# Attention and a gated feed-forward layer in f32: the first layer over 1024 tokens in 49 products instead of twice 26, two chunks of the second layer side by side, and the third batch's attention moved beside chunk 0

## Chip, cores and metric

One core of a Trainium2 chip. The time is the device time of one launch in microseconds (us). Engines: PE is TensorE (matmuls), PEld its weight loads, DVE is VectorE, ACT is ScalarE, POOL is GpSimd, SP is SyncE (it issues DMAs here).

## What is computed

```python
def _attn_ref(q, k, v, g_norm):                      # q, k, v: (8, 8, 576, 64)
    kv = np.einsum('bhsd,bhse->bhde', k, v)
    out = np.einsum('bhsd,bhde->bhse', q, kv)
    rms = np.sqrt(np.mean(out * out, axis=-1, keepdims=True) + 1e-06)
    return (out / rms * g_norm).astype(np.float32)
...
def _moe_ref(x, w_gate, w_val, w_out):               # x: (4608, 512), d_ff = 1536
    gate = 1.0 / (1.0 + np.exp(-(x @ w_gate)))
    val = x @ w_val
    return (gate * val @ w_out).astype(np.float32)
```

The attention output, heads side by side, is x: 8 batches of 576 tokens. The weights come in as f64, read as pairs of 32-bit words.

## The kernel before

**Tiles.** x is held transposed, features on partitions, in a ring of three chunks of `G` = 512 tokens (`xT_ring`). There are `NG` = 9 chunks, while batches have 576 tokens, so batch b's attention has to be done shortly before chunk b. d_ff is cut into `N3` = 3 groups `j`, each of four blocks of 128.

**Chunk 0** is computed plainly. `plain` (L618) makes gate and value with 512-column matmuls, ACT takes the sigmoid, DVE multiplies; `second` (L853) is the second layer. Beside it run the conversion of the weights to f32 (`convert`, L195 to L235: 18 units of 1024 columns, five DVE steps and two ACT steps each, staged by SP through three buffers), the attention of batch 1, the set-up of batch 2, and on POOL the sums of the first layer's weights (`w1_sums`, L770, 28 of 256 columns for each `j`). The order is written out by hand: `places` names steps after the n-th matmul (CV is one conversion step, LL loads k and v, W0 and W1 are weight sums, `t` turns q, `u` multiplies, `s` sums squares, `r` takes the root, `n` normalizes, `x` turns the result and sends it into the ring by SP's DMAs).

**Chunks 1 to 8** use a bilinear scheme. `PRODUCTS1` lists 26 products, which stand for a 4 x 4 by 4 x 2 block product (32 plain ones). Each names a PSUM bank region, a weight form, an x form and the steps after it. `first_layer_fast` (matmuls L977, two of 256 columns a product) runs the list for each `j`; `combine` gives a plain copy out of PSUM to ACT (L943) and every sum or difference to DVE (L947); POOL multiplies gate and value (L939; the last ones of `j` = 2 on DVE). Five PSUM banks go round (`free`). `second_layer_fast` (L1079) runs 26 products over sums of h (`h_sums`, L752, on POOL, some for `j` = 2 on DVE) and forms of the output weights. Forms of x are DVE subtractions (`x_sums`, L875 and L877), 18 per chunk. In chunk 1 the first layer reads its weight forms where they were made and SP stores them (`keep_w1`); from chunk 2 on POOL's DMA queue loads them back in four granules per `j` (L799), and 15 of the second layer's forms (L1035).

**Attention of batch c + 1** is spread over chunk c's products by `feed`: `kv_mm` and `u_mm` (L400, L450) on TensorE between products, turns (L416, L477), sums of squares (L462) and norms (L470) on DVE, square and root on ACT. `u_mm` borrows one of the five banks and a tile of three more.

Every engine works through its instructions in program order, so a step that is emitted between two products stands in that place in its engine's queue.

Of the kernel before, what the change touches and what calls it, by code (L numbers as in the profile page):

```python
# [20 lines left out]
def kernel(  # L21
# [55 lines left out]
    raw_ctx = tc.tile_pool(name="raw", bufs=1, side="right")  # L77
    raw = raw_ctx.__enter__()

    first_ctx = tc.tile_pool(name="first", bufs=4)  # L80
    first = first_ctx.__enter__()

# [4 lines left out]
    def load_kv(n):  # L87
        if n >= NE:
            return
        b, h0 = n // NHP, 2 * (n % NHP)  # L90
        for name, src in (("k", k), ("v", v)):
            t = first.tile([NP, 2, NJ * HD], FP32, tag=name, name=name)
            nc.sync.dma_start(out=t, in_=src[b, h0:h0 + 2].rearrange("h (p j) d -> p h (j d)", j=NJ))
            pairs[n][name] = t

    def load_q(n):
        h0 = 2 * n
        t = first.tile([NP, NJ, 2, HD], FP32, tag="q", name="q")
# [6 lines left out]
    def load_q_run(b, m):  # L105
        if b >= B:
            return
        if b == 1:
            t = h_main[2 - m].rearrange("p s c -> p (s c)")[:, 4 * NT * P - QW:4 * NT * P]
# [13 lines left out]
    def load_late(b):  # L123
# [5 lines left out]
        for n in range(NHP):  # L129
            for name, src in (("k", k), ("v", v)):  # L130
                mains[n, name] = t = kv_place(len(mains))
                (nc.gpsimd if b == 2 else nc.sync).dma_start(out=t.rearrange("p (h c) -> p h c", h=2),
                                  in_=src[b, 2 * n:2 * n + 2, 0:S4].rearrange("h (p j) d -> p h (j d)", j=NK4))
        rest = kv_place(len(mains))
        for i, src in enumerate((k, v)):
            for r in range(2):
                (nc.sync if b == 1 else nc.gpsimd if b == 2 else nc.scalar).dma_start(out=rest[PH * r:PH * r + PH, GH * i:GH * i + GH].rearrange("p (h d) -> p h d", d=HD),
# [11 lines left out]
    def load_unit(u, halves=(0, 1)):  # L149
# [3 lines left out]
        if 0 in halves:  # L153
            staged[u] = raw.tile([P, 2, DM], I64, tag="st", name="st", bufs=NST)
# [15 lines left out]

    EXP_OFF = 896
    one = const.tile([P, 1], FP32, name="one")
    nc.vector.memset(one, 1.0)
    exp_off = const.tile([P, 1], FP32, name="exp_off")
    nc.vector.memset(exp_off, -EXP_OFF * 2.0 ** 23)

    def convert(u):
# [24 lines left out]
        def s1():  # L202


            if u < 15:
                t = raw.tile([P, UW], U32, tag="cz", name="cz", bufs=2)
            else:
                t = at_ps()[:, 0:2].rearrange("p r c -> p (r c)").bitcast(U32)
            d["p"] = p = by_block(t)
# [50 lines left out]
    w1 = const.tile([P, N3, 4 * NMT, 2, P], FP32, name="w1")  # L260
    w2 = const.tile([P, NFT, DM], FP32, name="w2")
# [6 lines left out]
    kv_ahead = const.tile([P, NRUN, 2, HD], FP32, name="kv_ahead")  # L268
# [12 lines left out]
    NX = 3  # L281
    xT_ring = const.tile([P, NMT, NX * G], FP32, name="xT")
    xT = {c: xT_ring[:, :, G * (c % NX):G * (c % NX + 1)] for c in range(NG)}

    def chunk(c):
        return xT[c]
# [87 lines left out]
    def feed(b):  # L374
# [3 lines left out]
        def kv_mm(at, lent):  # L378
# [5 lines left out]
            def tails(first):  # L384
                for e in range(2):
                    for m in range(NRUN):
                        for g in range(2):
                            rs, c = slice(PH * m, PH * m + PH), HD * (2 * g + e)
                            nc.tensor.matmul(ps[m][HD * g:HD * g + HD, e], rest[rs, c:c + HD],
                                             rest[rs, GH + c:GH + c + HD], start=first and e == 0, stop=not first,  # L390
                                             skip_group_check=True)

            if b != 2:
                tails(True)
            for m in range(NRUN):
                for e in range(2):
                    for j in range(NK4):
                        for g in range(2):
                            c = slice(NK4 * HD * e + HD * j, NK4 * HD * e + HD * j + HD)
                            nc.tensor.matmul(ps[m][HD * g:HD * g + HD, e], mains[2 * m + g, "k"][:, c],  # L400
                                             mains[2 * m + g, "v"][:, c], start=(b == 2 and e == 0 and j == 0),
                                             stop=(b != 2 and j == NK4 - 1), skip_group_check=True)
            if b == 2:
                tails(False)

        def kv_set_aside():
            for m in range(NRUN):
                nc.scalar.copy(out=kv_ahead[:, m], in_=d["kv"][m])
            d["kv"] = [kv_ahead[:, m] for m in range(NRUN)]
# [13 lines left out]
        def heads_run(m):  # L423
# [13 lines left out]
            def u_mm(first=()):  # L437
                at = at_ps()
                d["u"] = u = at.rearrange("p r c -> p (r c)")[:, 0:2 * S]
                i_ = 4 if b == 1 else free.popleft()  # L440
# [13 lines left out]
            def u_square():  # L454
                i_, lent, to = d["lent"]
                nc.scalar.copy(out=to, in_=lent)
                if b > 1:
# [15 lines left out]
            def x_turn(i):  # L473
# [7 lines left out]
                for j in range(2):  # L481
                    for e in range(2):
                        p0, p1 = HD * e + QB * j, HD * e + QB * i
                        s0 = 0
                        while s0 < S // 2:
                            o = (S * b + S // 2 * j + s0) % (NX * G)
                            n_ = min(NX * G - o, S // 2 - s0)
                            nc.sync.dma_start(out=xT_ring[p1:p1 + QB, 2 * m:2 * m + 2, o:o + n_],
# [8 lines left out]
            if b == 1:  # L497
# [710 lines left out]
```

## Time and profile before

| | |
|---|---|
| runs | 999.07 and 1000.05 us, median 999.56 |
| profiled execution | 999.39 us, span 997.6, granted TensorE clock 1.000 |
| busy | PE 989.5, PEld 814.3, DVE 718.4, POOL 616.7, ACT 343.3 us |
| chunk 0 and start | to 156.67 us |
| a chunk with attention, first layer | 72.6 us |
| a chunk without, first layer | 67.34 us |
| second layer of a chunk | 33.68 us |
| DMA | 194.96 MB, mean 195 GB/s |

A stage's times are read from the chain of work that ended last and from busy times by stage. An f32 matmul leaves two records. Busy time of PE counts matmuls whose ends are modelled, so the gaps in the chain say more than the share. In a group's row the durations stand as busy time and mean in ns, then the engine's idle time ahead of the group and what ended it.

### The profile page before, as it was taken

The page shows a single profiled execution, that of the slowest core. Times are in us where ns is not written, and L with a number is a line of the kernel's source. Part 1 is how long each engine was busy: PE and PEld are TensorE (multiplying, and loading weights), DVE is VectorE, ACT ScalarE, POOL GpSimd, SP SyncE. Part 2 cuts the span into 40 slices and gives each one's busy share as a digit, 9 for nine tenths or more (in the row PEclk, how much of TensorE's full clock was granted, in tenths as well). Part 3 has the DMA queues.
Part 4 walks back from the last instruction along what each step waited for, and adds up shares of the span by engine and source line. Part 5 has one row for each costly group of instructions (what it writes and reads, how often), then busy time and mean ns, then how long its engine had stood idle before and what let it go on. Part 6 is the DMA issues. An engine that isn't in the chain of part 4 may idle for free.

```text
span 997.6 us, 16584 instructions
## 1 busy us (share of the span) xinstructions
PE 989.5 (99%) x5958; PEld 814.3 (82%) x5958; DVE 718.4 (72%) x1185; ACT 343.3 (34%) x621; POOL 616.7 (62%) x991
## 2 busy tenths in 40 slices
PE   8999999999999999999999999999999999999998
PEld 7455447888888888888888888888888888888887
DVE  4989999898768766784777576866687566756672
ACT  4576323661144213530344124511442133213320
POOL 1339997798259635865286708771686359734963
PEclk9999999999999999999999999999999999999999
DMA  9986415763989568746975677656954455545514
GB/s 273 304 235 207 150 42 148 232 217 100 295 269 291 154 195 273 198 157 200 277 225 162 198 212 260 181 168 198 279 178 146 147 188 197 159 148 168 215 49 123
DMA packets 149522, 194.96 MB, mean 195 GB/s; under 512 B 79840, under 2 KB 121696, under 8 KB 149440
## 3 DMA queue, kind: packets, MB, share of 16 engines
q0 software_dynamic: 22512, 116.41, 35.3%
q1 hardware_dynamic: 120848, 75.66, 26.9%
q10 hardware_dynamic: 6080, 1.84, 0.8%
q8 instruction: 47, 0.77, 0.3%
q14 instruction: 35, 0.29, 0.1%
HBM read 160.04 MB, written 25.56 MB: 186 GB/s over the span
## 4 chain that ended last, share of the span: by engine, by line
PE 91%; DVE 4%; ACT 2%; DMA 1%; issue 1%; SPq 0%; DVEq 0%; ACTq 0%
PE mm L977 54%; PE mm L1079 27%; PE mm L618 3%; PE mm L853 3%; PE at L450 2%; DVE w L222 1%; DVE cz L226 1%; DVE w L195 1%; PE at L400 1%; ACT sqs L494 1%; DMA v<-in_v_dram 1%; PE mm L400 1%; DVE cz L210 0%; ACT w L200 0%; DMA xT<-xTs 0%
## 5 line engine op out<-in xcount | busy, mean ns | idle before, releaser
L977 PE MATMUL mm<-xs,w 128*128 128x256 f32 x1428 | 331.2, 379 | 0.0
L977 PEld LDWEIGHTS mm<-xs,w 128*128 128x128 f32 x1428 | 270.9, 190 | 37.0
L977 PE MATMUL mm<-xT,w 128*128 128x256 f32 x948 | 230.5, 380 | 0.0
L977 PEld LDWEIGHTS mm<-xT,w 128*128 128x128 f32 x948 | 179.6, 190 | 25.0 <-issue 0.5
L799 POOL DMA_DIRECT2D w<-kept x84 | 46.9, 559 | 203.0 <-PE mm L977 199.5
L947 DVE TENSOR_TENSOR sg<-sg,mm 128x512 f32<-128x512 f32 (+1 forms) x176 | 100.7, 599 | 87.3 <-PE mm L977 34.3
L1079 PE MATMUL mm<-w,h 128*128 128x256 f32 x630 | 142.9, 379 | 0.0
L1079 PEld LDWEIGHTS mm<-w,h 128*128 128x128 f32 x630 | 119.6, 190 | 16.4 <-POOL h L939 0.2
L943 ACT COPY temps<-mm 128x512 f32<-128x512 f32 (+1 forms) x128 | 66.0, 537 | 187.1 <-PE mm L1079 94.7
L939 POOL TENSOR_TENSOR h<-h,sg 128x512 f32<-128x512 f32 x72 | 96.7, 1361 | 43.9 <-ACT sg L936 28.1
L752 POOL TENSOR_TENSOR h<-h 128x128 f32<-128x128 f32 x216 | 109.7, 520 | 16.5 <-DVE h_more L752 13.1
L1079 PE MATMUL mm<-w,h_more 128*128 128x256 f32 x474 | 108.2, 379 | 0.0
L936 ACT ACTIVATE sg<-sg 128x512 f32<-128x512 f32 x96 | 59.7, 630 | 127.0 <-DVE sg L947 127.0
L1079 PEld LDWEIGHTS mm<-w,h_more 128*128 128x128 f32 x474 | 90.1, 190 | 12.2
L943 ACT COPY sg<-mm 128x512 f32<-128x512 f32 (+1 forms) x112 | 57.2, 510 | 87.8 <-PE mm L1079 45.3
L752 POOL TENSOR_TENSOR h_more<-h 128x128 f32<-128x128 f32 x120 | 58.6, 492 | 34.6 <-DVE h L939 30.3
L947 DVE TENSOR_TENSOR temps<-temps,mm 128x512 f32<-128x512 f32 (+1 forms) x96 | 59.4, 619 | 27.1 <-PE mm L1079 16.9
L947 DVE TENSOR_TENSOR temps<-mm,temps 128x512 f32<-128x512 f32 (+1 forms) x64 | 39.8, 622 | 52.8 <-PE mm L1079 23.9
L618 PE MATMUL mm<-xT,w 128*128 128x512 f32 x176 | 77.2, 595 | 0.1
L943 ACT COPY h<-mm 128x512 f32<-128x512 f32 x48 | 28.1, 586 | 129.9 <-PE mm L977 116.4
L947 DVE TENSOR_TENSOR sg<-mm,sg 128x512 f32<-128x512 f32 (+1 forms) x64 | 39.6, 619 | 41.9 <-PE mm L1079 21.8
L618 PEld LDWEIGHTS mm<-xT,w 128*128 128x128 f32 x176 | 32.8, 190 | 40.0 <-issue 37.3
(154 smaller groups left out, 1293.0 us busy)
## 6 DMA issues: line engine op xcount, KB each, us to landing
w<-kept POOLq DMA_DIRECT2D x42, 896.0 KB, 5.3
w<-kept POOLq DMA_DIRECT2D x90, 384.0 KB, 4.5
w<-kept POOLq DMA_DIRECT2D x42, 768.0 KB, 5.0
out_dram<-sg SPq DMA_DIRECT2D x119, 64.0 KB, 1.7
q<-in_q_dram SPq DMA_DIRECT2D x96, 72.0 KB, 5.3
xT<-xTs SPq DMA_DIRECT2D x96, 72.0 KB, 4.8
st<-in_moe_w_gate_dram SPq DMA_DIRECT2D x12, 512.0 KB, 5.3
st<-in_moe_w_val_dram SPq DMA_DIRECT2D x12, 512.0 KB, 6.5
```

What stands on the lines that cost most here:

```text
L400: nc.tensor.matmul(ps[m][HD * g:HD * g + HD, e], mains[2 * m + g, "k"][:, c], mains[2 * m + g, "v"][:, c], start=(b == 2 and e == 0 and j ...
L450: nc.tensor.matmul(to[HD * e:HD * e + HD], qTs[HD * g:HD * g + HD, c:c + HD], kvq[HD * g:HD * g + HD, m, e], start=True, stop=True)
L618: nc.tensor.matmul(self.ps[i], w[("wg", "wv")[i], self.f][:, m, :], xT[self.c][:, m, :], start=(m == 0), stop=(m == NMT - 1), skip_group_c ...
L752: ops.append((eng, lambda v=v, x=x, sign=sign, y=y, eng=eng: eng.tensor_tensor(out=h_form(v, j), in0=h_form(x, j), in1=h_form(y, j), op=op ...
L799: nc.gpsimd.dma_start(out=granule(g)[:, 0:n], in_=kept1[g // NPA % N3, g % NPA][:, 0:n])
L853: nc.tensor.matmul(ps[t], gv[0, f][:, P * t:P * t + P], w["wo", f], start=(f == 0), stop=(f == NFT - 1), skip_group_check=True)
L936: nc.scalar.activation(out=o["o" + step[1]], in_=o["o" + step[1]], func=AF.Sigmoid)
L939: mult.tensor_tensor(out=o[x], in0=o[x], in1=o[y], op=ALU.mult)
L943: nc.scalar.copy(out=o[out_], in_=o[expr])
L947: tt(out=o[out_], in0=o[x], in1=o[y], op=ALU.add if sign == "+" else ALU.subtract)
L977: nc.tensor.matmul(regions[name][1][:, g], ws[:, g], xf[c][wv], start=(new and g == 0), stop=True, skip_group_check=True)
L1079: nc.tensor.matmul(regions[name][1], h_form(hv, j), ws[:, j], start=(used[i] and j == 0), stop=(j == N3 - 1), skip_group_check=True)
```

## The change

- The first layer takes two chunks at a time (`first_layer_super`, four pairs, chunks 1 to 8). The block product is now 4 x 4 by 4 x 4 in two nested levels of seven products: 49 for each `j`. A round is one outer product `i` (order `OUTER`) with its seven inner ones (`CYCLE`), of which two run in the next round. Inner products accumulate along three chains, each in one PSUM bank, read after every product: ACT copies a first touch where `i` is 1 or 5, all else is a DVE add into gate and h tiles.
- All weight forms of the first layer (49 blocks for each `j`) are made in chunk 0 by fewer and larger POOL sums, stored by SP, and loaded in pieces of five and two blocks into a ring of `NZ` = 16 blocks by POOL, for every pair, the first included. All 26 weight forms of the second layer are stored in pair 0 and loaded for every pair.
- The second layer (`second_layer_super`) runs each product for both chunks; its sums and copies are 512 wide instead of 256.
- Batch 2's attention runs whole in chunk 0. Pair s carries batches 3 + 2s and 4 + 2s (`where`, A and B); the last pair has none.
- x forms are 16 wider subtractions per pair (`x_plan`); x has four slots; one large tile `big` is laid out by hand.

The diff, cut to its core:

```diff
-    NX = 3
-    xT_ring = const.tile([P, NMT, NX * G], FP32, name="xT")
+    NX = 4
+    xT_three = const.tile([P, 3, NMT, G], FP32, name="xT")
...
-            if b == 1:
+            if b <= NRUN:
                 norms = [lambda: nc.vector.reciprocal(ms, ms)] + [lambda r=r: norm(r) for r in range(NAT)]
...
+    OUTER = (1, 2, 5, 6, 3, 7, 4)
+    CYCLE = ((1, 0), (7, 1), (5, 0), (2, 0), (4, 1), (6, 0), (3, 0))
+    NSUP = (NG - 1) // 2
+    for r in range(N3 * NQ + 1):
...
+        for k_, behind in CYCLE:
+            if 0 <= r - behind < N3 * NQ:
+                first_order.append((r - behind, k_))
+    NZ = 16
...
+    def load_piece(piece):
+        r, behind = piece
+        j, i = r // NQ, OUTER[r % NQ]
...
+            nc.gpsimd.dma_start(out=kb(at, m), in_=row[:, KB * col:KB * (col + m)])
...
+    def w1_sums(j):
...
+            return [lambda: tt_(out=s[0], in0=a(1, 0), in1=a(1, 1), op=ALU.add),
+                    lambda: tt_(out=s[1], in0=s[0], in1=a(0, 0), op=ALU.subtract),
+                    lambda: tt_(out=s[2], in0=a(0, 1), in1=s[1], op=ALU.subtract),
+                    lambda: tt_(out=s[3], in0=a(0, 0), in1=a(1, 0), op=ALU.subtract)]
...
+        outer = [lambda: tt_(out=A22, in0=A21, in1=A22, op=ALU.add),
+                 lambda: tt_(out=A21, in0=A11, in1=A21, op=ALU.subtract),
+                 lambda: tt_(out=A11, in0=A22, in1=A11, op=ALU.subtract),
+                 lambda: tt_(out=A12, in0=A12, in1=A11, op=ALU.subtract)]
+        return [pair_of(0, at[0], (1, 2), False), single(1, 1, at[1], 4), (outer, []),
+                pair_of(0, at[2], (6, 3), True), pair_of(1, at[3], (7, 5), True)]
...
+        def inner(st):
+            b = stacks[st]
+            t1, t2, t4 = xd_in[st]
+            return [sub(t1, b[:, :, 0, 1], b[:, :, 0, 0]), sub(t2, b[:, :, 1, 1], t1), sub(t4, b[:, :, 1, 0], t2),
+                    sub(b[:, :, 0, 1], b[:, :, 1, 1], b[:, :, 0, 1])]
+        outer = [sub(T3, B22, B12), sub(T1, B12, B11), sub(T2, B22, T1), sub(T4, B21, T2)]
+        i0, i1, i2 = inner(0), inner(1), inner(2)
+        return form, i1[:2] + outer + i1[2:] + i2 + i0
...
+        25:CV,W0,W,W,W,W,W,W,W,W 26:CV,CV 29:1u0,LL2 30:CV 31:1q0 32:CV,1t10,1s00,1s01,1r0 34:1rc0,CV,1n00 35:CV,K,K
+        36:CV,1t11,1n01,K,K 37:1n02,K,K 38:CV,K,K 39:W,W,W,W 40:CV,CV 41:CV,1x00 42:W,W,W,W 43:1x01 44:1u1 45:W,W,W,W 46:CV 47:1q1
+        48:CV,CV,CV,2t00 50:CV,1s10 52:CV,CV,2t01 54:1s11 55:CV,CV,1r1 57:CV,CV 58:CV,K,K 59:K,K
...
+        84:2x00 86:2x01 87:2u1,CV 89:2q1 91:2s10 93:2s11 94:2r1
+        96:2rc1,2n10 97:2n11,W2,W,W,W,W,W,W,W,W 98:2n12,K,K 99:K,K 100:2x10,K,K 101:K,K 102:2x11,K,K 103:K,K 105:P00,P10,P01
+        113:K,K 114:K,K,X,X 115:K,K,X 116:K,K,X 117:X 118:W,W,W,W 119:W,W,W,W,X
+        120:W,W,W,W,X 122:X 123:X 125:X 126:X 128:X 129:X 130:X
...
+    CHAIN = {1: 0, 6: 0, 7: 0, 4: 0, 5: 1, 3: 1, 2: 2}
+    TO = {1: (0, 0), 2: (0, 0), 6: (0, 1), 3: (0, 1), 7: (1, 1), 5: (1, 1), 4: (1, 0)}
...
+            for g in range(2):
+                nc.tensor.matmul(ps[:, g], ws[:, g], x, start=(new and g == 0), stop=True, skip_group_check=True)
...
+            if i == 1 or i == 5:
+                o = C21 if i == 1 else C22
+                if first:
+                    nc.scalar.copy(out=o, in_=ps)
+                else:
+                    tt(out=o, in0=o, in1=ps, op=ALU.add)
+            elif i == 2 or i == 3:
+                o, base = (C11, C21) if i == 2 else (C12, C22)
+                tt(out=o, in0=base if first else o, in1=ps, op=ALU.add)
+            else:
+                tt(out=C21, in0=C21, in1=ps, op=ALU.add)
...
+            mult = nc.vector if j == N3 - 1 else nc.gpsimd
+            if full and i == 2:
+                posts.append((p + 6, lambda o=C11: nc.scalar.activation(out=o, in_=o, func=AF.Sigmoid)))
+            elif full and i == 3:
+                tt(out=C12, in0=C12, in1=C21, op=ALU.add)
+                posts.append((p + 4, lambda o=C12: nc.scalar.activation(out=o, in_=o, func=AF.Sigmoid)))
+            elif full and i == 7:
+                tt(out=C22, in0=C22, in1=C21, op=ALU.add)
+                posts.append((p + 2, lambda o=C22, y=C12: mult.tensor_tensor(out=o, in0=o, in1=y, op=ALU.mult)))
+            elif full and i == 4:
+                posts.append((p + 2, lambda o=C21, y=C11, mult=mult: mult.tensor_tensor(out=o, in0=o, in1=y, op=ALU.mult)))
...
+            if h_fill and p % 2 < (2 if p % 7 < 3 else 1):
+                h_fill.popleft()[1]()
...
+                for half in range(2):
+                    nc.tensor.matmul(regions[name][1][:, half], h_form(hv, j)[:, half], ws[:, j],
+                                     start=(used[i] and j == 0 and half == 0), stop=(j == N3 - 1), skip_group_check=True)
...
+    where = """
+        0:A.t00 4:A.t01 25:A.u0 26:A.q0 28:A.t10 30:A.s00,A.s01 37:A.r0 39:A.t11 47:A.n00,A.n01 53:A.x00,A.x01 54:A.u1
+        56:A.q1,A.s10,A.s11 60:A.r1 61:A.n10 63:A.n11 66:A.x10,A.x11
+        30:BL 71:B.t00 75:B.t01 90:B.u0 91:B.q0 93:B.t10 95:B.s00,B.s01 102:B.r0 104:B.t11 112:B.n00,B.n01 118:B.x00,B.x01 119:B.u1
+        121:B.q1,B.s10,B.s11 125:B.r1 126:B.n10 128:B.n11 131:B.x10,B.x11
+    """
...
+            for n in range(len(W_SUMS)):
+                at1.setdefault(4 + 2 * n, []).append(w2_step(1))
```

## The prediction

> **What bounds the kernel now.** I read the page's busy table first, then the chain that ended last, the busy time by stage, VectorE's groups with shapes kept apart, and VectorE's timeline. All sums are made against the profiled execution: 999.39 us, of which the span is 997.6; the median of the runs is 999.56. A measurement of this kernel can tell about 2% (20 us) from no change.
>
> ```profile
> PE 989.5 (99%) x5958; PEld 814.3 (82%) x5958; DVE 718.4 (72%) x1185; ACT 343.3 (34%) x621; POOL 616.7 (62%) x991
> ```
>
> TensorE is the bound nearly everywhere. The chain says how tightly:
>
> ```profile
> 120.40 1.21 DVE w L235
> ...
> 127.25 1.64 DVE w L235
> 128.94 27.73 PE mm L853 x64
> 156.67 22.45 PE mm L977 x104
> ...
> 892.67 67.34 PE mm L977 x312
> 960.01 33.68 PE mm L1079 x156
> ```
>
> One f32 matmul leaves two records, so a first layer without attention is 156 matmuls of 256 columns in 67.34 us and a second layer 78 in 33.68: 0.4317 us each, with no gap. A product of the first layer (two halves, `g`) is 0.863 us. But before 128.94, in chunk 0, the chain runs from 62 us on mostly through VectorE (DVE): the conversion of the weights, L195 to L235. The stages say the same:
>
> ```profile
> 57.50:93.00 35.50, 35.50 (x370) 19.22 (x371) 32.78 (x36) 25.95 (x48) 26.07 (x26) 1.00 0.77 228
> 93.00:128.90 35.90, 35.80 (x83) 15.22 (x81) 33.71 (x33) 14.59 (x30) 35.27 (x27) 1.00 0.43 139
> 128.90:156.67 27.77, 27.73 (x65) 12.43 (x66) 27.34 (x28) 8.46 (x9) 27.14 (x31) 1.00 0.17 56
> 366.70:439.30 72.60, 72.60 (x538) 63.71 (x537) 53.91 (x90) 31.23 (x51) 43.24 (x73) 1.00 0.76 229
> ```
>
> After start:end and length, the columns are busy us of PE, PEld, DVE, ACT, POOL. From 57.5 to 156.67 DVE idles only 2.7 + 2.2 + 0.4 = 5.3 us: chunk 0 is as full on DVE as on TensorE. A later chunk (last row) leaves DVE 18.7 us in 72.6.
>
> **What the change takes away.** 1024 tokens took 52 products per `j`, now 49. Three products x 3 `j` x 2 halves = 18 matmuls x 0.4317 = 7.77 us per pair of chunks, four pairs: **-31.1 us**. The second layer keeps its 156 matmuls per pair. Batch 2's output matmuls (2 x 1.14 us, L450) move from chunk 1 into chunk 0: nothing in the sum, 2.3 us between stages.
>
> **First layer, what VectorE must do.** The rows for one add:
>
> ```profile
> L947 DVE TENSOR_TENSOR sg<-sg,mm 128x512 f32<-128x512 f32 x120 | 78.1, 684 | 61.2 <-PE mm L977 34.3 <-ACT temps L943 21.8
> L947 DVE TENSOR_TENSOR h<-h,temps 128x512 f32<-128x512 f32 x72 | 54.2, 753 | 0.8
> ...
> L462 DVE TENSOR_REDUCE ms<-sqs 128x9 f32<-128x576 f32 x28 | 19.8, 746 | 13.2 <-ACT sqs L459 13.2
> L477 DVE STREAM_TRANSPOSE xTs<-sqs 128x512 f32<-128x512 f32 x28 | 19.4, 693 | 0.0
> L416 DVE STREAM_TRANSPOSE qTs<-q 128x576 f32<-128x576 f32 x24 | 18.4, 770 | 8.8 <-PE mm L450 8.8
> ```
>
> Queued adds overlap a little. Two starts lie 0.60 us apart:
>
> ```profile
> 381.02 0.68 DVE L947 TENSOR_TENSOR h<-temps,mm 128x512 f32<-128x512 f32 x1
> 381.62 0.68 DVE L947 TENSOR_TENSOR sg<-mm,sg 128x512 f32<-128x512 f32 x1
> ```
>
> So I take 0.60 for an add that reads PSUM and, by the 753 ns row, 0.68 for one with both inputs in SBUF. By the new code a round of seven products (6.04 us of TensorE) gives DVE 3 adds where `i` is 1 or 5 (ACT copies the first touches), 7 where `i` is 2, 6 or 4, and 11 where `i` is 3 or 7 (7 x 0.60 + 4 x 0.68 = 6.9 us). Per `j` that is 49 adds, where two chunks had 42, ACT's copies falling from 18 to 8. An average of 72% would be harmless; the order is not. Products 1, 6, 7, 4 of a round accumulate in one bank, each waits until DVE has read the one before, and only two others (1.73 us) lie between. With 0.60 us for the add and some 0.15 for two handovers (0.06 us from L235's end to the matmul at 128.94), DVE may be late by about 1 us; what it is later, TensorE waits.
>
> I carried the lag product by product (add 0.863, take off DVE's due work). The same count on the old product list gives no wait, as the trace has it. On the new list:
> - `j`=0, rounds 3 and 7 with batch A's `t10`, `s00`, `s01`, `t11` between them: 6.9 + 6.9 + 0.7 + 1.3 + 0.7 = 16.5 us against 12.1. Less the slack, and spilling into the next round: 2.9 us.
> - the end of `j`=2: rounds 3, 7, 4 (18.0 us) and six of the eight gate products, which there run on DVE (4.1), against 19.9 us. And the last round has nothing to lie between: 7 follows 3 after one product, 4 follows 7 at once, so TensorE waits out the adds and what is queued ahead of them. 5.0 us; with B's `n10`, `n11`, `x10`, `x11` in the same stretch 9.2.
> - elsewhere 0.5 to 1 us.
>
> Pairs 0 and 1 carry two batches (12.7 us each), pair 2 one (8.5), pair 3 none (6.0): **+40 us**. With adds at 0.58 and 0.60 the count gives 29, with 0.62 and 0.75, 51.
>
> **Chunk 0.** Four things come onto DVE, which has nothing to spare there.
> - Batch 2: 4 turns x 0.70, 4 sums x 0.66, 2 reciprocals x 0.2, 4 output turns x 0.75 = 8.9 us.
> - The forms of x for 1024 tokens: 16 subtractions with 4 x 1024 + 4 x 768 + 8 x 512 elements. At the spacing of uncontended adds (0.34 for 256 elements, 0.60 for 512) 12.8 us, against 18 x 0.34 = 6.1 before: 6.7.
> - POOL's sums. How POOL slows DVE is seen in one conversion before and during POOL's W0, and in one x sum:
>
> ```profile
> 66.07 0.69 DVE L195 TENSOR_SCALAR w<-st 128x1024 uint32<-128x1024 uint32 x1
> 69.13 1.21 DVE L226 SCALAR_TENSOR_TENSOR cz<-st,cz 128x1024 uint32<-128x1024 uint32 x1
> ...
> 89.12 1.21 DVE L195 TENSOR_SCALAR w<-st 128x1024 uint32<-128x1024 uint32 x1
> 93.13 1.75 DVE L226 SCALAR_TENSOR_TENSOR cz<-st,cz 128x1024 uint32<-128x1024 uint32 x1
> ...
> 151.42 0.94 DVE L875 TENSOR_TENSOR xs<-xT 128x256 f32<-128x256 f32 x1
> ...
> 367.91 0.43 DVE L875 TENSOR_TENSOR xs<-xT,xs 128x256 f32<-128x256 f32 x1
> ```
>
> A unit costs 5.1 us alone (66 to 71 us), 7.0 beside POOL (89 to 96): 10.5 units x 1.9 + 18 x sums x 0.5 = 29 us lost to 84 POOL sums of 256 elements. The new sums are 20 per `j`, 60 in all, but of 11,264 elements per `j` where it was 7,168. If the loss goes by elements it grows by 16.6 us, if by instructions it falls by 8. I take +10, nearer the first: both engines' times grow with the elements (POOL 0.73 us for 256, 1.28 for 512).
> - What DVE can win back of the 5.3 us idle: 0 to 5, taken as 2.5.
>
> Together 8.9 + 6.7 + 10 - 2.5 = 23 us later, of which 2.3 is covered by the TensorE work moved here: **+21 us** (0 to 30). What is late next is the first layer itself: its adds stand behind the x forms in DVE's queue, and TensorE's banks run out after eight products.
>
> The Trainium skill, "SBUF — State Buffer", section "Who interferes with whom", says that VectorE with two SBUF inputs and GpSimd hold the shared port for whole instructions, while an add with one input in PSUM contends with nobody. The rows agree on the second (684 ns whatever POOL does). By the first, the loss goes by elements, and chunk 0 would be +27 instead of +21.
>
> **Priced at nothing or nearly.** The 26 weight blocks of the second layer and all 49 of the first now come from DRAM through POOL (896 KB landed in 5.3 us, issue 0.56): a block of the ring of 16 is needed again about 11 products (9.5 us) after it is free, 3.6 us to spare. In pair 0 POOL has 15 sums of 768 elements (1.8 us each, 27 us) within 30 us of products, and a load stands behind them: +1 (0 to 8). Queued behind a load that waits for TensorE are gate products and h sums. The stores of the new weights go to SP, ahead of staging loads; three staging buffers hide them, some 14 us (two conversions); without them every us late is a us of chunk 0. The side-by-side second layer halves DVE's instructions and stays under TensorE's 67.3 us; its start is covered by 16 matmuls (6.9 us) against some 7 us of late gates and sums on DVE.
>
> **Sum.** 999.4 - 31.1 + 40 + 21 + 1 = **1030 us**. Ends: 999.4 - 31.1 + 29 + 0 = 997 and 999.4 - 31.1 + 51 + 30 + 8 = 1057.
>
> **Rivals.**
> 1. *DVE keeps up and only TensorE's saving is seen.* For it: DVE's 72%, and that the old list, by the same count, bears a lag of 4 us at the end of a `j`. Against: the shared bank with two products between. It decides if the rounds' lag stays under about 1 us. With a half-grown chunk 0 at most: 968 to 980, say 975. Faster.
> 2. *The layers hide their adds, chunk 0 doesn't*: 999.4 - 31.1 + 21 = 989, up to 1005 with the waits at the ends of `j`=2 alone (4 x 5 us less some). No change.
> 3. *The weight loads come late.* POOL in `j`=1: 28 h sums x 0.75 to 0.9, 8 gates x 1.3, 16 loads x 0.56 = 40 to 45 us of 42. If it falls behind by over 3.6 us, TensorE waits for weights, some 8 us per pair on top of half the rest: 1060 to 1080.
>
> **Chances.** My forecast (997 to 1057) 0.62, rival 1 0.11, rival 2 0.17, rival 3 0.10. The range runs from 988, which leaves out rival 1 and part of rival 2, to 1062. Over 2% faster is below 979.4: rival 1 but for its edge, 0.09. Within 2% is up to 1019.4: rival 2 and the low end of mine, 0.27. Slower: 0.64.
>
> **What would show it.** Right: first layers of about 145 us with two batches and 133 with none, with waits of TensorE for DVE adds in rounds 3 and 7 and at the end of `j`=2; the first layer of the new form starting near 178 us rather than 157, with DVE over 95% busy up to it. Wrong: 49 x 3 products in 127 us without a gap (then 1), waits of TensorE for `kept` loads (then 3), or conversions that cost 5 us beside POOL.

## The result, and the profile after

The changed kernel takes **1124.03 us** (two runs, 1122.19 and 1125.86) against 999.56 before: a ratio of 1.1245, 95% interval 1.1163 to 1.1327. Forecast were 1030 us, from 988 to 1062: the direction was right, the size far too small. The profiled execution has a span of 1124.0 us.

The page's busy line:

```profile
PE 1007.1 (90%) x5814; PEld 800.5 (71%) x5814; DVE 798.8 (71%) x1070; ACT 271.4 (24%) x463; POOL 635.3 (57%) x777
```

TensorE fell from 99% to 90%, while VectorE's share hardly moved: nothing is busier than before, so engines wait for each other. Busy time by stage (start:end and length, then busy us of PE, PEld, DVE, ACT, POOL, and the granted TensorE clock): chunk 0, the first layers of pairs 0 to 3, and between them one second layer.

```profile
0.00:190.91 190.91, 164.67 (x1095) 85.90 (x1095) 161.26 (x166) 92.03 (x174) 113.67 (x85) 0.94 0.91 258
190.91:386.98 196.07, 151.62 (x1036) 124.55 (x1037) 145.83 (x206) 47.47 (x74) 135.36 (x143) 0.91 0.75 229
386.98:456.34 69.36, 69.36 (x314) 60.72 (x313) 40.32 (x48) 5.28 (x9) 34.77 (x51) 0.97 0.46 143
456.34:619.80 163.46, 145.15 (x1037) 121.10 (x1036) 126.17 (x196) 45.92 (x72) 83.50 (x116) 0.98 0.68 192
...
688.80:839.61 150.81, 138.39 (x813) 116.08 (x812) 115.59 (x174) 36.95 (x60) 83.17 (x116) 0.98 0.58 172
...
907.94:1049.19 141.25, 131.04 (x590) 111.21 (x588) 105.07 (x152) 27.91 (x48) 83.12 (x116) 0.99 0.49 154
```

What each first layer would take without new waits follows from the rows of before: two old first layers (72.6 us with attention, 67.34 without) less 7.8 us for the three products saved. That is 137.4 for pairs 0 and 1, 132.2 for pair 2, 126.9 for pair 3. The excess is 58.7, 26.1, 18.6 and 14.3 us; chunk 0 is 34.2 us later than before; the second layers of pairs 0 to 2 are 1 to 2 us each over 67.35. The forecast had 13.7, 12.7, 8.5 and 6.0 for the pairs, 21 for chunk 0 and nothing for the second layers. An excess holds more than waits for adds: other waits are in it, and matmuls at a lower clock.

**The waits that were forecast are there.** This is TensorE's timeline at the end of pair 3's first layer (start, us, line; in brackets the idle time before and what ended it):

```profile
1044.77 1.13 PE L1010 MATMUL mm<-big 128*128 128x256 f32 x4 [1.99 <-DVE big L1026]
1047.32 2.07 PE L1010 MATMUL mm<-big 128*128 128x256 f32 x4 [1.42 <-DVE big L1026]
```

The last two products wait 1.99 and 1.42 us for VectorE's adds. The second one then takes 2.07 us. The windows of 2 us say why (busy PE, then the granted clock):

```profile
1046.00:1048.00 2.00, 0.68 (x2) 0.60 0.00 0
1048.00:1050.00 2.00, 2.00 (x6) 0.50 0.00 0
```

The clock falls during the second wait and is at half from 1046.4 to 1053.2, well into the second layer. At the ends of pairs 1 and 2 it falls before the second wait begins (at 616.3 and 834.8, the second waits at 616.6 and 837.0), and in pair 1 one wait of 2.4 us for a load of v, with no other wait near it, is followed by half clock as well:

```profile
PE at L382 <- DMA big<-in_v_dram: 2.4, 1, 2.4
...
484.34:486.34 2.00, 2.00 (x58) 0.50 0.30 52
```

Summed over such windows of the whole run, (1 - clock) x length is 43.8 us: 11.9 in chunk 0, 16.7 in pair 0's first layer, 15.2 in the rest. That is the most it can have cost, as TensorE stands still in some of this time anyway. The kernel before has 1.00 throughout, and the prediction had no term for this.

**Pair 0 starts with a pile-up.** VectorE's last x forms and POOL's last first-layer sums, from the two timelines:

```profile
197.25 9.97 DVE L860 TENSOR_TENSOR big<-big 128x768 f32<-128x768 f32 x4
...
191.15 2.87 POOL L811 TENSOR_TENSOR big<-big 128x1024 f32<-128x1024 f32 x1 [5.20 <-DMA kept<-big]
```

Two lines of the waits, with total, times and longest: TensorE's in this first layer, and POOL's in the whole run.

```profile
PE mm L1010 <- DVE big L1021: 10.9, 2, 10.5
POOL big L811 <- DMA kept<-big: 38.3, 3, 20.6
```

Four forms take 9.97 us beside POOL's wide sums, and TensorE waits 10.5 us for the first add behind them (at 208.54). POOL is so late because its sums wait for stores (38.3 us at L811 in all) that stand in SP's queue behind staging loads, q loads and x sends. Next, TensorE stands 6.8 us at 221.91 (a weight piece issued only behind the last sum) and 11.5 us at 259.08 (an add behind a VectorE form at L1100, which waits for a POOL sum at L1098, which waits for a store).

### The profile page after: what moved, and what is told of

The parts are those of the page before. It is cut to its first block, busy times and chain, and to the rows that moved or that the text cites. A ratio compares the mean times of both kernels' runs of the same rounds, so it can differ in the third digit from the quotient of the medians.

```text
span 1124.0 us, 16075 instructions
## 1 busy us (share of the span) xinstructions
PE 1007.1 (90%) x5814; PEld 800.5 (71%) x5814; DVE 798.8 (71%) x1070; ACT 271.4 (24%) x463; POOL 635.3 (57%) x777
## 4 chain that ended last, share of the span: by engine, by line
PE 49%; DVE 20%; DMA 12%; POOL 9%; SPq 5%; issue 4%; ACT 0%; DVEq 0%; POOLq 0%; ACTq 0%
PE mm L1126 25%; PE mm L1010 22%; DVE big L1026 8%; DVE big L1033 3%; DVE big L1024 3%; DMA big<-in_v_dram 3%; DMA kept<-big 3%; SPq L122 2%; DVE big L1036 2%; DMA big<-in_moe_w_val_dram 2%; DMA big<-in_moe_w_out_dram 1%; POOL big L783 1%; DMA big<-kept 1%; POOL big L780 1%; POOL big L706 1%
## 5 line engine op out<-in xcount | busy, mean ns | idle before, releaser
L1010 PE MATMUL mm<-big 128*128 128x256 f32 x1776 | 425.8, 389 | 46.6 <-DVE big L1026 42.9
L1010 PEld LDWEIGHTS mm<-big 128*128 128x128 f32 x1776 | 337.5, 193 | 114.2 <-DVE big L1026 62.3
L706 POOL TENSOR_TENSOR big<-big 128x256 f32<-128x256 f32 x304 | 230.4, 776 | 96.6 <-DVE big L1039 85.7
L1126 PE MATMUL mm<-big 128*128 128x256 f32 x1248 | 276.7, 385 | 0.0
L1126 PEld LDWEIGHTS mm<-big 128*128 128x128 f32 x1248 | 242.5, 194 | 34.6
L755 POOL DMA_DIRECT2D big<-kept x196 | 108.3, 553 | 162.7 <-PE mm L1010 133.2
L1026 DVE TENSOR_TENSOR big<-big,mm 128x512 f32<-128x512 f32 x252 | 168.7, 682 | 40.8 <-PE mm L1010 35.9
L1010 PE MATMUL mm<-xT,big 128*128 128x256 f32 x576 | 150.1, 390 | 35.9 <-DVE big L1024 17.2
L1024 DVE TENSOR_TENSOR big<-big,mm 128x512 f32<-128x512 f32 x168 | 114.2, 682 | 55.0 <-PE mm L1010 51.3
L1010 PEld LDWEIGHTS mm<-xT,big 128*128 128x128 f32 x576 | 110.0, 194 | 57.5 <-DVE big L1024 21.6
L1019 ACT COPY big<-mm 128x512 f32<-128x512 f32 x96 | 56.3, 586 | 320.9 <-PE mm L1010 308.3
L1072 POOL DMA_DIRECT2D big<-kept x104 | 56.9, 547 | 90.0 <-PE mm L1126 89.6
L976 DVE TENSOR_TENSOR big<-big,mm 128x512 f32<-128x512 f32 x44 | 29.8, 685 | 85.4 <-PE mm L1126 85.3
L589 PE MATMUL mm<-xT,big 128*128 128x512 f32 x192 | 86.4, 607 | 0.1
L1021 DVE TENSOR_TENSOR big<-big,mm 128x512 f32<-128x512 f32 x72 | 49.2, 685 | 43.9 <-PE mm L1010 41.1
L972 ACT COPY big<-mm 128x512 f32<-128x512 f32 x36 | 21.1, 586 | 205.1 <-PE mm L1126 205.1
L589 PEld LDWEIGHTS mm<-xT,big 128*128 128x128 f32 x192 | 36.5, 194 | 44.9 <-issue 41.8
L1037 POOL TENSOR_TENSOR big<-big 128x512 f32<-128x512 f32 x32 | 41.3, 1291 | 31.3 <-DVE big L1036 27.7
L918 PE MATMUL mm<-big 128*128 128x512 f32 x96 | 45.8, 636 | 7.1 <-DVE big L229 6.2
```

What stands on the lines that cost most here:

```text
L589: nc.tensor.matmul(self.ps[i], w[("wg", "wv")[i], self.f][:, m, :], chunk(self.c)[:, m, :], start=(m == 0), stop=(m == NMT - 1), skip_grou ...
L706: ops.append((eng, lambda v=v, x=x, sign=sign, y=y, eng=eng: eng.tensor_tensor(out=h_form(v, j), in0=h_form(x, j), in1=h_form(y, j), op=op ...
L755: nc.gpsimd.dma_start(out=kb(at, m), in_=row[:, KB * col:KB * (col + m)])
L918: nc.tensor.matmul(ps[t], gv[0, f][:, P * t:P * t + P], w["wo", f], start=(f == 0), stop=(f == NFT - 1), skip_group_check=True)
L1010: nc.tensor.matmul(ps[:, g], ws[:, g], x, start=(new and g == 0), stop=True, skip_group_check=True)
L1019: nc.scalar.copy(out=o, in_=ps)
```

## Experiments

Times are of one run, or medians where a ratio stands beside them; the kernel before ran on the same chip each time and took 999.1 to 1000.2 us. The changed kernel and its relatives scatter by 4 to 8 us from run to run (four runs of e15 took 1101.2 to 1109.4), so smaller differences are not read. The stages are those of the profiled executions; a pair here is its first and second layers together (before: two chunks), the last one with the tail.

| run | us | chunk 0 | pair 0 | pair 1 | pair 2 | pair 3 |
|---|---|---|---|---|---|---|
| before | 999.6 | 156.7 | 210.1 | 212.5 | 212.4 | 205.9 |
| changed | 1124.0 | 190.9 | 265.4 | 232.5 | 219.1 | 216.1 |
| e7_no_extra | 1065.6 | 193.2 | 252.5 | 211.5 | 203.7 | 202.7 |
| e13_pool_adds | 1131.4 | 191.8 | 264.4 | 228.2 | 222.7 | 222.2 |
| e5_pool_gates | 1110.6 | 189.1 | 262.3 | 228.7 | 214.5 | 214.2 |
| e4_fill | 1097.7 | 190.8 | 258.1 | 222.2 | 212.9 | 209.4 |
| e2_memset | 1105.5 | 181.3 | 259.0 | 229.0 | 218.0 | 216.2 |
| e11_no_stores | 1106.9 | 199.4 | 238.9 | 232.2 | 218.8 | 215.5 |
| e14_no_w1 | 1081.2 | 175.1 | 240.6 | 228.7 | 218.4 | 216.2 |
| e8_no_w2 | 1110.2 | 189.5 | 254.5 | 231.1 | 219.3 | 213.9 |
| e12_all_off | 1006.3 | 170.0 | 212.6 | 216.3 | 204.1 | 201.5 |
| e15_three_repairs | 1101.6 | 191.4 | 263.2 | 223.2 | 212.6 | 209.3 |
| e9_pool_adds_fill | 1105.1 | 190.3 | 258.0 | 223.2 | 217.8 | 216.0 |
| e3_no_b2 | 1121.0 | 184.9 | 263.6 | 229.7 | 225.1 | 216.0 |
| e1_stores_act | 1153.4 | 210.2 | 271.5 | 232.0 | 218.6 | 219.3 |
| e10_stores_pool | 1156.8 | 204.1 | 283.8 | 232.3 | 218.9 | 215.7 |

### The adds

**e7_no_extra**

```diff
-                tt(out=C12, in0=C12, in1=C21, op=ALU.add)
...
-                tt(out=C22, in0=C22, in1=C21, op=ALU.add)
```

> The changed kernel without the eight adds of each j in the first layer that join two inner results in SBUF (C12 = C12 + C21 and C22 = C22 + C21 where i is 3 or 7: four in each of the two rounds; 24 a pair of chunks); the values of those tiles lack a term. If the first layers wait because VectorE falls behind in the rounds 3 and 7 (11 adds in 6.04 us of TensorE), taking 4 x 0.8 to 0.9 us from each of these rounds ends nearly all waits in the middle of a j, and shortens those at its end: pairs 1 to 3 each shorter by 6 to 12 us, the kernel by 20 to 40. If the waits come from the accumulating bank itself (a product has to wait for the add that reads the one before, whatever VectorE's load is), the waits stay: 0 to 8 us in all.

1065.59 us, 58.4 less than the changed kernel: half as much again as the theory's upper end. First layers of pairs 1 and 3, by stage:

```profile
445.67:589.81 144.14, 139.22 (x1037) 120.24 (x1036) 106.88 (x172) 45.82 (x72) 82.06 (x116) 1.00 0.76 217
860.86:991.13 130.27, 127.68 (x590) 111.47 (x588) 86.96 (x128) 27.91 (x48) 81.72 (x116) 1.00 0.53 167
```

The largest group of TensorE's waits in pair 1, in the changed kernel and then here:

```profile
PE mm L1010 <- DVE big L1026: 12.3, 11, 2.0
...
PE mm L1010 <- DVE big L1026: 2.8, 2, 1.4
```

With those for L1024, TensorE's waits for VectorE's adds in pair 1 fall from 15.8 to 3.6 us; the clock is 1.00 in pairs 1 to 3, and all second layers before the last take 67.3 us. Eight adds in 49 products decide: without them VectorE keeps up in rounds 3 and 7. So the load is the cause, and the accumulating bank alone (the rival) costs little.

**e13_pool_adds** puts the same adds on POOL (`nc.gpsimd.tensor_tensor`), with nothing left out.

> The changed kernel, complete, with the 24 adds a pair that join two inner results in SBUF on POOL instead of VectorE (1.28 us for 512 elements there, 0.82 to 0.94 here). Leaving them out gave 58.5 us. If VectorE's load in rounds 3 and 7 is the cause, most of this comes back: 1070 to 1090, with VectorE's other work slowed a little and gate products later. If the waits only pass to POOL (31 us more a pair; gates, sums of h and weight loads stand behind these adds), 1095 to 1130, with waits of TensorE for POOL or for weight loads.

1131.40 us: the rival's result, just above its range. VectorE's waits, by line and releaser (us in total, times, longest):

```profile
DVE big L1026 <- POOL big L1036: 42.2, 8, 6.3
DVE big L1026 <- POOL big L1033: 28.0, 12, 3.4
```

The next round adds into the same tile (C21) that POOL is still reading, so VectorE's queue stops behind POOL's. Work moved off the busy engine without moving it out of the chain.

**e5_pool_gates** puts the gate products of `j` = 2 on POOL (`mult = nc.gpsimd`).

> The changed kernel with the gate products of j = 2 on POOL too, instead of on VectorE (eight of 512 elements a pair, some 5 us of VectorE's work at the end of each first layer). If VectorE's queue sets the waits at the end of j = 2 (four gaps of 1.3 to 2 us, and the halved clock after them), the ends of all first layers get 2 to 4 us shorter, 8 to 16 in all. If the last gates on POOL (1.3 us each, behind sums of h and weight loads) come later than VectorE would give them, the second layers start late: 0 to 12 us more in all, as waits of TensorE or VectorE for POOL at the start of the second layer.

1110.57 us, 13.5 less (one run): as the theory had it. Second layers start at full clock in pairs 1 and 2 (67.3 us).

### The ends of the first layers, and the clock

**e4_fill** puts two products of the second layer (`j` = 0 and 1) between the last three of the first:

```diff
-        for i in (0, 1, 2, 6):
+        for i in (2, 6):
             product(i, some)
...
+        for p, i in ((N1 - 3, 0), (N1 - 2, 1)):
+            at1.setdefault(p, []).append(lambda i=i: begun[3](i, range(N3 - 1)))
```

> Two products of the second layer (their blocks j = 0 and 1, 1.7 us each) are put between the last three products of the first layer, which wait for DVE's adds one after the other. If the waits there cost TensorE time twice, in the wait (3.4 us a pair) and in the halved granted clock after it (some 2 to 3 us a pair): 4 to 6 us for each of four pairs, 1100 to 1108, and the second layers at 67.5 us instead of 69. If DVE is the bound there, the wait only moves to the start of the second layer, where the forms of j = 2 are late: 0 to 1 us a pair, 1120 to 1125.

1097.68 us, ratio 1.097 (1.0891 to 1.1049): 26 us back, a little more than the first theory's 16 to 24. The same place as shown above:

```profile
1018.32 1.89 PE L1119 MATMUL mm<-big 128*128 128x256 f32 x8
1020.48 1.13 PE L1010 MATMUL mm<-big 128*128 128x256 f32 x4 [0.27 <-DVE big L1026]
```

The waits of 1.99 and 1.42 us are gone but for 0.27, and from 384 us on no window of 2 us has a clock below 1.00. TensorE's waits for L1026 fall from 42.9 to 31.3 us in the whole run. What came back beyond these 11.6 us is mostly the clock, of which 15.2 us at most were lost behind pair 0's first layer.

**e16_before_gaps** takes the *kernel before* and puts waits of known size into a stage that has none:

```diff
+                stall = {(0, 8): 1, (1, 8): 1, (1, 9): 1, (2, 3): 4, (2, 13): 1, (2, 14): 1, (2, 15): 1}.get((j, i), 0)
+                if c == NG - 1 and stall:
+                    junk, x = pair(sqs[:, 0:G]), xf[c][PRODUCTS1[i + 1][2]]
+                    nc.vector.tensor_copy(out=junk, in_=regions[name][1])
+                    for _ in range(stall):
+                        tt(out=junk, in0=junk, in1=junk, op=ALU.add)
+                    nc.vector.tensor_copy(out=x[:, 0:1], in_=x[:, 0:1])
```

> The kernel before, its results unchanged, with waits put into the first layer of its last chunk, where TensorE has none: after chosen products VectorE copies the bank, does some adds on a scratch tile and touches the next product's x form, so that TensorE waits some 1.5 to 2 us (about 4 us at one place). One wait alone in j = 0, two with one product (0.86 us) between in j = 1, one of about 4 us and later three with one product between each in j = 2. If the granted clock answers to waits that stand close together (in the changed kernel two waits of 1.99 and 1.42 us with 1.1 us of work between were followed by a clock of 0.5 for some 6 us, single ones of 1.3 to 1.7 us by none), j = 0 keeps 1.00, the pair and the three are followed by 0.5, costing some 3 us each beyond the waits: 14 to 16 us of waits and 6 to 9 us of halved clock, 1020 to 1025 in all. If the clock's fall in the changed kernel has another cause, it stays at 1.00 throughout and only the waits are paid: 1013 to 1017.

1026.38 us, ratio 1.0262 (1.0232 to 1.0292), just above the range with a falling clock. TensorE's waits sum to 16.1 us, yet 26.2 us are lost. The single wait, the pair, and the first of the three, then the clock after each:

```profile
902.55 1.99 PE L977 MATMUL mm<-xs,w 128*128 128x256 f32 x8 [1.64 <-DVE xs L985]
927.10 1.10 PE L977 MATMUL mm<-xs,w 128*128 128x256 f32 x4 [1.83 <-DVE xs L985]
930.94 2.08 PE L977 MATMUL mm<-xs,w 128*128 128x256 f32 x4 [2.73 <-DVE xs L985]
...
968.90 1.10 PE L977 MATMUL mm<-xT,w 128*128 128x256 f32 x4 [1.66 <-DVE xT L985]
```

```profile
903.00:905.00 2.00, 2.00 (x11) 1.00 0.28 115
...
931.00:933.00 2.00, 2.00 (x5) 0.50 0.95 356
...
971.00:973.00 2.00, 1.43 (x3) 0.50 0.00 0
```

One wait of 1.64 us leaves the clock alone. Waits of 1.83 and 2.73 us with one product between them halve it until about 936, a lone one of 4.97 us until about 960, three of about 1.6 us, one product apart, until 981. So waits make the clock fall, in a kernel where nothing else was changed; the 10.1 us lost beyond the waits fit 23.9 us at half clock. That three waits of about 1.6 us do what one of 1.64 us didn't shows that it matters how close they stand. The pair shows less, as its 2.73 us may have been enough alone: in the changed kernel 2.4 us were.

### Chunk 0 and pair 0

**e11_no_stores** and **e2_memset**, alone and together (**e14_no_w1**):

```diff
# e11: no stores of first-layer forms; loads of the same size from q
-            return lambda: nc.sync.dma_start(out=out, in_=in_)
+            return lambda: None
...
-        row = kept1[:, j, ROW[i]]
+        row = instead[:, NQ * KB * ((NQ * j + ROW[i]) % 10):]
# e2: the 60 sums of first-layer weights
-        tt_ = nc.gpsimd.tensor_tensor
+        def tt_(out, in0, in1, op):
+            nc.gpsimd.memset(out, 0.01)
```

> The 60 POOL sums that make the first layer's weight forms are replaced by POOL memsets of the same places, so POOL no longer reads SBUF there; the forms' values are left out, every store, load and wait stays. Port theory: DVE's conversions beside them fall from about 7 us a unit to 5, the first layer starts some 20 us earlier (170 us) and the x forms ahead of pair 0 take 13 us instead of 20: 1085 to 1095 in all. Queue theory: POOL is shorter, but the waits for the stores stay: the start moves by under 10 us, and the whole to 1108 to 1118.

1105.5 us: chunk 0 is 9.6 us shorter. From 31.5 to 190.9 VectorE is busy 20.6 us less (123.7 for 144.3), but in that stretch it now waits 20.3 us for staging loads (5.7 in the changed kernel), and POOL 61.0 us for stores. So the start moved as the queue theory had it, and the total came out just below its range. The two causes stand behind each other.

> The changed kernel without the stores of the first layer's weight forms (SP issues none of them, POOL's sums wait for none); the loads of the same sizes read rows of q in DRAM instead, so that the values of those forms are others. Up to the first product of the new first layer the changed kernel has 161.3 us of VectorE work and 29.7 us of VectorE idle, against 136.3 and 20.4 in the kernel before. Theory: the idle part, and POOL's 38 us of waiting for stores (which pushes the last sums into pair 0, beside the x forms), come from the stores in SP's queue, which I priced at nothing. Then chunk 0 ends 8 to 16 us earlier (175 to 183), and pair 0, freed of the x forms' 10.5 us and the late weight load, is 10 to 20 us shorter: 1090 to 1105. Rival: VectorE's added work sets chunk 0, and what the stores delay is hidden: chunk 0 within 4 us of 191, pair 0 within 6 of 196, 1114 to 1125.

1106.86 us. The total is near the theory, but not the split: chunk 0 became 8.5 us *longer*, since POOL's sums, held up no more, now all fall on the conversions there; pair 0 is 26.5 us shorter. This shows that the stores cost time by pushing POOL's sums into pair 0.

> The changed kernel without the stores of first-layer weight forms (loads read rows of q) and with the first layer's weight sums as memsets; all else is there. One by one, the suspects bring 17.3 us (stores), 18.5 (sums), 13.9 (second-layer weights) and 58.5 (adds), 108 together, but all at once 117.8. If sums and stores take each other's place (as the run with memsets showed: POOL then waits 61 us for stores and VectorE 20 for staging), the missing 9.6 us lie between these two: 1124.0 - 17.3 - 18.5 - 9.6 = 1079, with chunk 0 near 170. If they lie with the other two, this run is at 1088 or a little over, with pair 0 held by something else.

1081.17 us, near the 1079 of the first case: sums and stores do take each other's place. Together they bring 42.9 us, alone 18.5 and 17.2. These are single runs, so the stages say it more clearly: chunk 0 changes by -9.6 and +8.5 us with one of them out and by -15.8 with both. The forms that took 9.97 us, here:

```profile
171.38 3.80 DVE L863 TENSOR_TENSOR big<-big 128x768 f32<-128x768 f32 x4
```

**e8_no_w2** leaves the second layer's weight sums out:

```diff
...
+        w2_keeps.extend([keep(v) for v in range(8)])
+        return
```

> The changed kernel without the 15 sums and the VectorE forms of the second layer's weights in pair 0 (the eight raw blocks are still stored, and the loads take raw blocks in place of the sums). Theory: pair 0's +61 us over its matmuls is mostly this set-up: x forms slowed beside POOL's sums (10.5 us), a first-layer weight load issued behind the last sum (6.8), and a VectorE form that waits for a POOL sum that waits for a store (11.5), with the halved clock after each. Then pair 0's first layer falls from 196 us by 25 to 40 us, to 156 to 171, near pair 1's 163.5, and the other stages stay. Rival: pair 0 is late because all that chunk 0 left over is still queued (x forms, stores on SP, attention loads), and the set-up of the second layer only waits beside it: 0 to 12 us.

1110.22 us; pair 0's first layer falls by 9.8 us only: the rival. The x forms still take 9.98 us and TensorE still waits 8.7 us behind them, since their neighbour on POOL is the first layer's sums.

**e3_no_b2** leaves batch 2's attention out but for the sends.

> Batch 2's attention is left out of chunk 0 (its loads of q, k and v, turns, matmuls, sums and norms); only the sends of its result stay, which send batch 1's once more. DVE-work theory, as in the prediction: the first layer starts 11 us earlier (8.9 us of DVE and 2.3 of TensorE), pair 0 is unchanged: about 1112. Queue theory: SP also loses 16 q loads of 0.6 to 1.5 us, so the stores and staging loads behind them come earlier and the start moves by 15 to 25 us, with pair 0 shorter too: 1095 to 1108.

1121.04 us, as neither theory had it: chunk 0 is only 6 us shorter, with POOL's wait for stores up to 43.8 us, and the total is within the scatter.

**e1_stores_act** and **e10_stores_pool** issue all weight stores on ACT's or POOL's queue instead of SP's.

> All stores of weight forms (first and second layer) go out from ACT's DMA queue instead of SP's. Queue theory: in chunk 0 and pair 0 POOL's in-place sums wait for stores that stand in SP's queue behind q loads and x sends (POOL waited 38 us for them, and 11 us in pair 0), and DVE and TensorE stand behind POOL. Then the first layer starts before 180 us instead of at 191, its first pair takes under 175 us instead of 196, and the whole some 1080 to 1100 us. Port theory (POOL's wide sums slow DVE at the shared SBUF port, the stores are idle time that costs nothing): no gain, 1119 to 1129. Against both: a store on ACT that waits for a POOL sum holds up the conversion steps behind it, which could cost 5 to 15 us in chunk 0.

> The changed kernel with all stores of weight forms (first and second layer) issued by POOL on its own DMA queue instead of by SP. Theory: in chunk 0 the stores stand in SP's queue behind and ahead of staging and q loads, and POOL's sums wait for them (38 us at one tile) and VectorE for staging; on POOL's queue, behind the sums that they store, they wait for nobody. Then chunk 0 ends 8 to 12 us earlier (near 180) and pair 0 falls by 8 to 12 us: 1100 to 1108 in all. Rival: SP's order isn't what sets the end; POOL pays 86 issues x 0.56 us = 48 us and its sums come later still: no gain, or up to 25 us more.

1153.38 and 1156.75 us: both slower. On ACT the stores hold up its copies (TensorE waits 33.3 us for L1019); on POOL they hold up what stands behind them (a weight load of pair 0 is issued at 244.69, behind the last sums and twelve stores of 7.4 us together, and TensorE stands 36.2 us until 253.95). Neither is a clean test of SP's queue, as each makes a new one. e11 takes the stores away altogether, so it shows what they cost, but not whether any queue could carry them better.

### All at once, and what can be had back

**e12_all_off** combines the edits of e11, e2, e8 and e7.

> The changed kernel with all four suspects left out at once: no stores of first-layer weight forms (loads read rows of q), the first layer's weight sums on POOL as memsets, no sums of second-layer weights, and none of the 24 adds a pair that join two inner results in SBUF. If these four are the whole of the excess, but for the waits at the ends of j, what is left is chunk 0 at about 165 us (VectorE's 136 of before, 15.6 for batch 2 and the wider x forms, and its idle time), pair 0's first layer about 145 like pair 1's in the run without the adds, then 144, 136 and 130 with second layers of 67.3: 985 to 1005 in all. If something else holds pair 0 or chunk 0 back (loads of k, v and q, TensorE's own order), it stays above 1015.

1006.26 us, just above the range: the four account for 117.8 of the 124.5 us by which the change is slower.

**e9_pool_adds_fill** and **e15_three_repairs** leave nothing out.

> A complete version with three repairs: two products of the second layer between the last three of the first (alone 26 us), the gate products of j = 2 on POOL (alone 13.6 us) and the 24 adds a pair on POOL too. If the three add up (the adds bringing 35 to 50 us), 1035 to 1060; as the first two and the adds work on the same waits at the end of j = 2, 1050 to 1070 is likelier. If POOL can't carry gates and adds, 1080 to 1110. In no case does it come near 1000 us, as chunk 0 and pair 0 keep some 80 us of their excess.

> A complete version with three repairs that each need nothing left out: two products of the second layer between the last three of the first (alone 26 us), the gate products of j = 2 on POOL (alone 13.6 us) and the sums of the second layer's weights in pair 0 begun 18 products later (out of the way of the first round's weight loads and of the stores still in SP's queue; leaving them out altogether gave 13.9 us, so 3 to 10 here). Gates and fill work on the same waits at the end of j = 2: 1080 to 1092. If the late weight sums make pair 0's second-layer forms late, or the gates on POOL wait behind them: 1092 to 1105.

1105.14 us (ratio 1.1059, 1.1008 to 1.111) and 1101.61 us (1.1036, 1.0992 to 1.108). Neither beats the fill alone: where that covers the last adds, gates on POOL bring nothing more (pairs 1 to 3 of e15 and e4), and with later weight sums pair 0 is 5 us longer, which is within the scatter. No version that computes everything comes near the kernel before. Even with the adds left out, pairs 1 to 3 win only 1.0, 8.7 and 3.2 us over it, while chunk 0 and pair 0 lose 36 and 42.

## Why the prediction was right or wrong

The direction and the places were right, but the sum was 94 us short. Pair 0's first layer is 45 us of that (an excess of 58.7 for 13.7), the first layers of pairs 1 to 3 are 32 (59.0 for 27.2) and chunk 0 is 13; the rest lies in the second layers.

- **TensorE's saving, -31.1 us: right.** Without the extra adds, pair 2's first layer takes 136.4 and pair 3's 130.3 us, 3 to 4 us over the matmul time with the saving in it.
- **Waits for adds: mechanism and place right, price too low.** TensorE's measured waits for adds are 15.8, 11.4 and 9.8 us in pairs 1 to 3, against 12.7, 8.5 and 6.0. The reason stands in VectorE's groups:

```profile
L1026 DVE TENSOR_TENSOR big<-big,mm 128x512 f32<-128x512 f32 x252 | 168.7, 682 | 40.8 <-PE mm L1010 35.9
L1033 DVE TENSOR_TENSOR big<-big 128x512 f32<-128x512 f32 x48 | 45.2, 943 | 1.7
L1036 DVE TENSOR_TENSOR big<-big 128x512 f32<-128x512 f32 x48 | 39.4, 820 | 1.7
```

  An add that reads PSUM takes 682 ns as before, but one with both inputs in SBUF 943 and 820 where I carried 0.68 us, from a row of 753. Less the 0.07 that I had taken off for overlap, that is 0.3 to 0.8 us more in each of the rounds 3 and 7, some 3.2 a pair, which is the size of the gap. The means hide two prices: of these 96 adds, the 64 with no POOL sum or product beside them take 0.69 us each, the other 32 take 1.26. The prediction counted on POOL slowing VectorE in chunk 0, but not here, and the row of 753 was such a mean already. The excess of a pair holds more than these waits: in pair 1, 26.1 us are 15.8 of waits for adds, 2.4 for a load of v and 7.9 of neither, which the next point bears on. The prediction's sign "first layers of about 145 us with two batches" doesn't follow from the sum either, which gives 137.4 + 12.7 = 150; measured were 163.5 in pair 1.
- **The clock: a missing term.** I read the 1.00 in the stages of before as a constant, where TensorE hardly ever waits. The Trainium skill, "TensorE: Matmul & The Clock Gate", section "HAM oscillation — how this bites in real kernels", has the rule that TensorE must not idle for more than some 3.4 us. The trace agrees that waits halve the clock, but shorter ones do it too: 1.99 and 1.42 us at the ends of first layers, 2.4 us once with no other wait near, and in e16 three of about 1.6 us. The Trainium skill's same page, section "A second HAM failure mode: psum-queue depth-cycling", comes nearer: short idle spells between groups of matmuls make the clock go up and down.
- **Chunk 0, +21 us: too low by 13.** Up to the end of the x forms (161.9 before, 207.2 after) VectorE is busy 35.9 us longer (177.4 for 141.5), where the terms 8.9 + 6.7 + 10 make 25.6. The term of +10 for POOL's wider sums failed: with the other two as priced, it was 20, and the conversions alone take 17 us longer. The loss by elements that the prediction sets beside the Trainium skill's "SBUF — State Buffer", section "Who interferes with whom", gave 16.6: nearer, and still low. With the sums as memsets and no stores (e14) that work ends at about 175 us.
- **VectorE's idle time, -2.5 us: wrong in sign.** Up to the first new product it rose from 20.4 to 29.7 us; 6.7 of the added 9.3 are waits of the conversions (L193) for staging loads, of which the kernel before had none.
- **Stores on SP "priced at nothing": wrong, and behind the largest miss, pair 0.** "Three staging buffers hide them" took only the staging loads into account. The sums that overwrite a stored block wait for the store, 38 us, and that moves POOL's last sums beside the x forms and the first round of pair 0. That the first layer's adds stand behind the x forms was said, but had no price; TensorE waits 10.5 us there. Without the stores pair 0 is 26.5 us shorter and chunk 0 8.5 longer; with sums and stores both out, chunk 0 and pair 0 together are 40.6 us shorter.
- **Weight loads, +1 (0 to 8): in its range as a direct wait** (6.8 us at one place in pair 0). Rival 3 did not happen: waits of TensorE for `kept` loads stay below 1 us in pairs 1 to 3.
- **The new first layer near 178 us, VectorE over 95% busy up to it:** it started at 190.9, with VectorE 84% busy from the start and 89% from 60 us on. That it was not full was the sign that its conversions waited.

## What to carry to other kernels

Count the work of a round against the round, not against the stage: here eight adds in two rounds of a `j` cost 58 us, where the three products saved in a `j` brought 31. Where a bound engine begins to wait, price the clock with the wait, put other work between products that wait, and do it first at the end of a stage. Follow a buffer from writer through store to the next writer before a store is called free, and when two causes stand behind each other, take out both before judging either.

## What the hardware showed that was not expected

- The granted TensorE clock of one core falls to 0.50 after waits of 1.6 to 2.7 us, for 3.4 to 10.2 us at a time. In the kernel before with added waits, three of about 1.6 us with one product between them are followed by 10.2 us at half, a single one of 1.64 us by none. In the changed kernel single waits of 1.0 to 1.7 us leave the clock at 1.00, and a single one of 2.4 us is followed by 3.4 us at half. No run finds the border between them: in e11 the clock is at half from 536.0, behind a single wait of 1.66 us.
- A VectorE add of 512 elements with both inputs in SBUF takes 0.69 us with no POOL sum or product beside it and 1.26 on average with one; an add that reads PSUM takes 0.68 either way.
- A VectorE subtraction of 768 elements, both inputs in SBUF, takes 0.95 us a piece without POOL's sums (3.80 us for four) and 2.49 us beside sums of 1024 and 512 elements (9.97 for four).
